# Causal attention feeding a two-layer MoE: pinned order with MoE matmuls between the attention parts, shared PSUM banks, contiguous Q/K copies

## The chip, the cores and the metric

The kernel runs on one core of one Trainium2 chip. The metric is the device time of one execution in microseconds (us), given as the median of several executions. Every experiment was timed in turns with the kernel before on the same chip. PE is TensorE (its matmuls), PEld its weight loads, DVE is VectorE, ACT ScalarE, POOL GpSimd, SP SyncE. "Clock" is the mean TensorE clock that the records say was granted, where 1.00 is full speed. A matmul is called "warm" when 512 columns take 216 ns from start to start, as they do in the tail of these traces, and "cold" when they take twice that (426 ns). PSUM is the memory that this kernel's matmuls write to; the program hands it out in banks, and has a bank written anew only when the last reader of its old content is done.

## The reference

```python
B, H, S, Nb, D = (8, 8, 576, 16, 64)
k_all = np.concatenate([beacon_k, k], axis=2)          # 16 beacon rows ahead of 576
v_all = np.concatenate([beacon_v, v], axis=2)
scores = scale * np.matmul(q, k_all.transpose(0, 1, 3, 2))
scores = np.where(causal, -1000000000.0, scores)       # beacon columns are never masked
a = np.exp(scores - scores.max(-1, keepdims=True))
a /= a.sum(-1, keepdims=True) + 1e-09
x = np.matmul(a, v_all).transpose(0, 2, 1, 3).reshape(B * S, H * D)   # 4608 x 512
h = x @ w_in                                           # 512 -> 2048
out = np.maximum(0.01 * h, h) @ w_out                  # 2048 -> 512
```

Two heads make a *pair*; there are 32 pairs. The MoE works on chunks of 512 tokens. A *step* of the steady part does one pair of attention, 16 MoE matmuls of the first layer (moe1: four groups of four) and 16 of the second (moe2: one sum of 16).

## The kernel before

Only what the change and the argument touch; "..." marks cuts.

```python
ps_sc = ... tile_pool(name="ps_sc", bufs=2, space=PSUM)    # scores, 2 banks each
ps_mb = ... tile_pool(name="ps_mb", bufs=2, space=PSUM)    # Q, K, x transposes and values
ps_acc = ... tile_pool(name="ps_acc", bufs=2, space=PSUM)  # MoE sums
...
def load_beacon_k(b):                                      # for each of 8 batches
    for e in range(2):
        nc.gpsimd.dma_start(out=bk[:, e, :], in_=beacon_k[b]...)   # casting load
    ps = ps_mb.tile(...); nc.tensor.transpose(ps[:, 0:128], ...); nc.vector.tensor_copy(out=bkT[:, b]..., in_=ps[:, 0:128])
...
def transposes(g):
    ...
    for par in range(2):
        nc.gpsimd.tensor_copy(out=kT[ps_, 0:NB], in_=bkT[ps_, b, 2 * hp + par, :])
    for src, dst in ((q_nat, qT), (k_nat, kT[:, NB : NB + S])):
        ps = ps_mb.tile([128, 1024], BF16, name="mb", tag="mb")
        for i in range(RI):                                # RI = 6 transposes of 96 rows
            nc.tensor.transpose(...)
        nc.vector.tensor_copy(
            out=dst.rearrange("c (p i) -> c i p", i=RI),   # writes hop by 6 elements
            in_=ps[:, 0:S].rearrange("c (i p) -> c i p", i=RI),
        )
...
for g in range(NG + 2):
    ...                       # loads of the next batch, two weight pieces
    transposes(g)
    if 1 <= g <= NG:
        scores(g - 1)         # 4 parts: 12 matmuls, exp on ACT
    if g >= 2:
        values(g - 2)         # 30 matmuls in two halves, x_nat, 5 transposes, copy to xT
    if g >= NPAIR + 2:
        moe_step(g - NPAIR - 2)   # 4 x moe1 (4 matmuls, Prelu on ACT), then moe2 (16 matmuls)
for m in range(NG - NPAIR, NPAIR * (NCH + 1)):
    moe_step(m)               # 12 steps of MoE alone: the tail
```

The order of the instructions on each engine is not this program order: a scheduler decides it. It puts nearly all MoE matmuls at the end of a step and leaves one or two between attention parts.

The softmax here doesn't subtract the row's maximum and nothing guards it: scores larger than these inputs give would overflow.

## Time and profile before

| | before |
|---|---|
| time, median of 4 runs beside the kernel after | 523.54 us (521.84 to 524.33) |
| span of the profiled execution | 522.0 us |
| mean granted clock | 0.928 |
| PE busy | 407.5 us, so 114.5 us idle |
| first step with moe2 begins at | 128.28 us |

To read it, cut the span in two at the begin of the first step that has both MoE layers. Up to there is the *start* (128.3 us), after it the *rest* (393.7 us): 24 steps with attention and both MoE layers, the last two short of a part, and the tail of 12 steps of MoE alone. The first is TensorE's largest waits over the whole execution (total us, times, longest us); the second the rows of the page for PE and its clock, in 40 slices of the span; the third the two copies:

```profile
PE mb L261 <- DVE qT L187: 35.3, 29, 1.5
PE mb L148 <- DMA bk<-in_beacon_k_dram: 34.0, 2, 17.5
PE mb L261 <- DVE kT L187: 21.9, 24, 1.1
PE sc L204 <- POOL kT L178: 6.7, 1, 6.7
```

```profile
PE   0103777887888888888888888888987889999996
PEclk9999999987888887998888998888799889999999
```

Of the 114.5 us that TensorE is idle, 57 are waits of the value matmuls for the bank that a Q or K copy still reads, and 41 (34.0 and 6.7) belong to the beacon at the start. The two copies themselves (busy us, mean ns):

```profile
L187 DVE COPY qT<-mb 128x576 bf16<-128x576 bf16 x32 | 66.4, 2075 | 9.6 <-PE mb L182 7.2
L187 DVE COPY kT<-mb 128x576 bf16<-128x576 bf16 x32 | 70.4, 2199 | 0.0
```

The clock row dips in most slices of the middle and stays up only in the tail.

### The profile page before, as it was taken

How to read it: one execution, taken by the hardware profiler on the slowest of the kernel's cores; microseconds unless marked ns; L12 is line 12 of the kernel's file. 1: busy time of each engine (PE TensorE's matmuls, PEld its weight loads, DVE VectorE, ACT ScalarE, POOL GpSimd, SP SyncE). 2: the span in 40 equal slices, each digit the busy share in tenths (PEclk: the TensorE clock that was granted, in tenths of full speed). 3: DMA queues.
4: the chain of work that ended last, by engine and by line, in shares of the span. 5: the costliest groups of instructions: out<-in, count | busy, mean ns of one | idle time of the engine just before them, and what ended most of it. 6: DMA issues, size and time to landing. Idle time of an engine off the chain costs nothing.

```text
span 522.0 us, 7381 instructions
## 1 busy us (share of the span) xinstructions
PE 407.5 (78%) x3048; PEld 208.6 (40%) x3048; DVE 239.3 (46%) x369; ACT 201.0 (39%) x305; POOL 115.7 (22%) x205
## 2 busy tenths in 40 slices
PE   0103777887888888888888888888987889999996
PEld 0102435443444444444444444444444445444443
DVE  1305768655455556555554556454355443100111
ACT  0001364555344443444444444534344345333310
POOL 4944344514050405031500331030000000000000
PEclk9999999987888887998888998888799889999999
DMA  9999946537070626217430700070000001011112
GB/s 217 204 266 193 175 95 43 103 88 49 1 202 21 57 35 164 60 27 65 121 102 21 67 21 21 20 68 21 0 23 35 5 21 41 21 41 40 41 40 82
DMA packets 63713, 38.10 MB, mean 73 GB/s; under 512 B 42688, under 2 KB 59072, under 8 KB 63680
## 3 DMA queue, kind: packets, MB, share of 16 engines
q0 software_dynamic: 45184, 9.31, 21.6%
q1 hardware_dynamic: 18496, 28.32, 19.2%
q8 instruction: 24, 0.39, 0.3%
q14 instruction: 9, 0.07, 0.0%
HBM read 37.49 MB, written 9.44 MB: 90 GB/s over the span
## 4 chain that ended last, share of the span: by engine, by line
PE 63%; DVE 24%; DMA 7%; issue 3%; ACT 1%; SPq 1%; POOL 0%; DVEq 0%; POOLq 0%
PE acc L293 26%; PE acc L305 24%; DVE kT L187 12%; DVE qT L187 9%; PE mb L261 7%; DMA bk<-in_beacon_k_dram 4%; PE sc L204 3%; PE mb L279 3%; DVE osb L313 2%; DMA v_aug<-in_v_dram 2%; DMA k_raw<-in_k_dram 1%; PE mb L182 1%; ACT aT L215 1%; SPq L131 1%; DVE aT L232 0%
## 5 line engine op out<-in xcount | busy, mean ns | idle before, releaser
L215 ACT ACTIVATE aT<-sc 128x928 bf16<-128x928 f32 (+2 forms) x128 | 105.3, 856 | 187.1 <-PE sc L204 186.8
L293 PE MATMUL acc<-xT,w_in_sb 128*128 128x512 bf16 x576 | 165.9, 423 | 0.0
L305 PE MATMUL acc<-w_out_sb,gT 128*128 128x512 bf16 x576 | 129.5, 379 | 0.0
L300 ACT ACTIVATE gT<-acc 128x512 bf16<-128x512 f32 x144 | 86.0, 597 | 112.5 <-PE acc L293 112.5
L313 DVE COPY osb<-acc 128x512 f32<-128x512 f32 x36 | 24.9, 692 | 188.6 <-PE acc L305 188.6
L261 PE MATMUL mb<-v_aug,aT 128*128 128x65 bf16 (+1 forms) x960 | 56.7, 217 | 64.6 <-DVE qT L187 35.3
L293 PEld LDWEIGHTS <-w_in_sb 128*128 128x128 bf16 x576 | 59.0, 108 | 63.7 <-issue 24.1
L305 PEld LDWEIGHTS <-gT 128*128 128x128 bf16 x576 | 56.4, 98 | 67.9
L261 PEld LDWEIGHTS <-aT 128*128 128x128 bf16 (+1 forms) x960 | 48.2, 112 | 82.9 <-issue 79.1
L187 DVE COPY qT<-mb 128x576 bf16<-128x576 bf16 x32 | 66.4, 2075 | 9.6 <-PE mb L182 7.2
L187 DVE COPY kT<-mb 128x576 bf16<-128x576 bf16 x32 | 70.4, 2199 | 0.0
L178 POOL COPY kT<-bkT 64x16 bf16<-64x16 bf16 x64 | 12.7, 199 | 198.1 <-PE sc L204 100.8
L204 PE MATMUL sc<-qT,kT 64*128 64x128 bf16 (+5 forms) x384 | 50.0, 335 | 8.2 <-POOL kT L178 6.7
L271 DVE TENSOR_TENSOR x_nat<-mb,rec 128x384 bf16<-128x384 f32 x64 | 31.3, 490 | 2.0
L137 POOL CAST q_nat<-q_raw 96x768 bf16<-96x768 f32 x28 | 22.7, 828 | 39.5 <-issue 38.8
L137 POOL CAST k_nat<-k_raw 96x768 bf16<-96x768 f32 x32 | 27.7, 889 | 5.9 <-DMA k_raw<-in_k_dram 5.9
L148 PE MATMUL mb<-ident,bk 128*128 128x128 bf16 x8 | 1.9, 242 | 34.0 <-DMA bk<-in_beacon_k_dram 34.0
L279 PE MATMUL mb<-ident,x_nat 128*128 128x128 bf16 (+1 forms) x160 | 24.9, 272 | 0.7 <-DVE x_nat L271 0.7
L204 PEld LDWEIGHTS <-kT 64*128 64x128 bf16 (+1 forms) x384 | 14.0, 105 | 28.3 <-issue 15.7
L279 PEld LDWEIGHTS <-x_nat 128*128 128x128 bf16 (+1 forms) x160 | 15.3, 126 | 18.9 <-DVE x_nat L271 10.5
L270 DVE RECIPROCAL rec<-mb 128x6 f32<-128x6 f32 x64 | 12.2, 190 | 23.3 <-PE mb L261 23.3
L160 POOL DMA_DIRECT2D v_aug<-in_v_dram x24 | 21.2, 893 | 4.7 <-DMA w_in_sb<-in_moe_w_in_dram 4.7
(28 smaller groups left out, 166.5 us busy)
## 6 DMA issues: line engine op xcount, KB each, us to landing
q_raw<-in_q_dram SPq DMA_DIRECT2D x32, 288.0 KB, 4.0
k_raw<-in_k_dram SPq DMA_DIRECT2D x32, 288.0 KB, 4.7
out_dram<-osb SPq DMA_DIRECT2D x36, 256.0 KB, 2.0
v_aug<-in_v_dram POOLq DMA_DIRECT2D x24, 128.0 KB, 4.9
w_in_sb<-in_moe_w_in_dram POOLq DMA_DIRECT2D x4, 512.0 KB, 19.6
w_out_sb<-in_moe_w_out_dram POOLq DMA_DIRECT2D x4, 512.0 KB, 13.8
v_aug<-in_v_dram POOLq DMA_DIRECT2D x8, 112.0 KB, 3.5
v_aug<-in_v_dram POOLq DMA_DIRECT2D x8, 80.0 KB, 4.5
```

The costliest lines, as they stand in the source:

```text
L137: eng.tensor_copy(out=dst[:, :, h0 + 2 * e : h0 + 2 * e + 2, :], in_=raw[:, 2 * e : 2 * e + 2].rearrange("p h i d -> p i h d"),)
L160: nc.gpsimd.dma_start(out=t[:, c, :, 0:D], in_=v[b, :, OFF[c] : OFF[c] + 128].rearrange("h p d -> p h d"),)
L187: nc.vector.tensor_copy(out=dst.rearrange("c (p i) -> c i p", i=RI), in_=ps[:, 0:S].rearrange("c (i p) -> c i p", i=RI),)
L204: nc.tensor.matmul(out=sc[0 : ROWS[c], par, col - c0 : col - c0 + w], lhsT=kT[ps_, c * 128 : c * 128 + ROWS[c]], rhs=qT[ps_, q0 : q0 + w], ...
L215: nc.scalar.activation(out=aT[:, :, c0 : c0 + w], in_=sc[:, :, 0:w], func=AF.Exp, scale=0.125)
L261: nc.tensor.matmul(out=avv[:, n, 0 : D + 1], lhsT=aT[0 : ROWS[c], par, a0 : a0 + 128], rhs=va[0 : ROWS[c], c, 2 * hp + par, :], start=(c = ...
L271: nc.vector.tensor_tensor(out=x_nat[:, t0:t1].rearrange("p t e d -> p (t e) d"), in0=avv[:, :, 0:D], in1=rec[:, n0:n1, None].to_broadcast( ...
L279: nc.tensor.transpose(ps[:, q0 : q0 + rows], x_nat[0:rows, t].rearrange("p e d -> p (e d)"), ident[0:rows, 0:rows],)
L293: nc.tensor.matmul(out=acc, lhsT=w_in_sb[:, j, fc * 128 : (fc + 1) * 128], rhs=xT[:, j, i * 512 : (i + 1) * 512], start=(j == 0), stop=(j ...
L300: nc.scalar.activation(out=gT[i][:, fc, :], in_=acc, func=AF.Prelu, alpha=0.01)
L305: nc.tensor.matmul(out=acc, lhsT=gT[i][:, fc, t * 128 : (t + 1) * 128], rhs=w_out_sb[:, fc, :], start=(fc == 0), stop=(fc == NF - 1),)
L313: nc.vector.tensor_copy(out=osb, in_=acc)
```

## The change

Its intent is to keep TensorE busy without gaps. It has five parts:

1. *Order.* The whole schedule is pinned to program order, and eight groups of four MoE matmuls stand between the attention parts of a pair. Q and K stay one pair ahead of the scores, as before, but the first pair is now transposed before the loop, so every pair comes one earlier against the weight loads.
2. *Banks.* The two PSUM pools of two banks become one pool of four single banks.
3. *Copies.* The Q/K copies write contiguously and take the hop on the PSUM side.
4. *Beacon K.* One plain load, one cast by POOL and eight transposes up front take the place of 16 casting loads.
5. *First loads.* Two heads first, and one load for each tensor.

```diff
-    ps_mb = ...(name="ps_mb", bufs=2, ...)
-    ps_acc = ...(name="ps_acc", bufs=2, ...)
+    ps_one = ...(name="ps_one", bufs=4, ...)
...
-    def load_beacon_k(b):
-        for e in range(2):
-            nc.gpsimd.dma_start(out=bk[:, e, :], in_=beacon_k[b].rearrange("h n d -> (h n) d"))
+    def load_beacon_k():
+        nc.scalar.dma_start(out=bk_raw, in_=beacon_k.rearrange("b h n d -> (h n) b d"))
+        nc.gpsimd.tensor_copy(out=bk, in_=bk_raw[:, :, None, :].to_broadcast([128, B, 2, D]))
...
-                out=dst.rearrange("c (p i) -> c i p", i=RI),
-                in_=ps[:, 0:S].rearrange("c (i p) -> c i p", i=RI),
+            out=dst.rearrange("c (p i) -> c p i", i=RI),
+            in_=ps[:, 0:S].rearrange("c (i p) -> c p i", i=RI),
...
+    def fill(m, n):                       # even n: one moe1 group; odd n: a quarter of moe2
+        i, part = divmod(m, NPAIR)
+        if m < 0: return
+        if n % 2 == 0:
+            if i < NCH: moe1(i, part * 4 + n // 2)
+        elif i >= 1: moe2(i - 1, part, n // 2)
...
+    order = tc.manual_schedule(engines={PE, Activation, DVE, Pool, SP})
+    with order:
...
+        for g in range(NG + 1):
+            m = g - NPAIR - 1
...
+            if has(g + 1): t_q(g + 1, 0)          # Q transposes and copy, one pair ahead
+            fill(m, 0)
+            if has(g + 1): t_q(g + 1, 1)          # K; its beacon columns copied by POOL
+            fill(m, 1)
+            if has(g): score(g, 0); score(g, 1)
+            fill(m, 2)
+            if has(g - 1): value(g - 1, 0)
+            fill(m, 3)
+            if has(g): score(g, 2); score(g, 3)
+            fill(m, 4)
+            if has(g - 1): value(g - 1, 1)
+            fill(m, 5)
+            fill(m, 6)
+            if has(g): masks(g)
+            if has(g - 1): x_transposes(g - 1)
+            fill(m, 7)
```

(Shortened: engine names stand without their prefix, and short conditions on one line.)

## The prediction

> **What bounds the kernel now.** I read the page's chain first, then the waits of TensorE in the steady part, then one table of stretches, then single instructions. The chain that ended last:
>
> ```profile
> PE 63%; DVE 24%; DMA 7%; issue 3%; ACT 1%; SPq 1%; POOL 0%; DVEq 0%; POOLq 0%
> PE acc L293 26%; PE acc L305 24%; DVE kT L187 12%; DVE qT L187 9%; PE mb L261 7%; DMA bk<-in_beacon_k_dram 4%; PE sc L204 3%; PE mb L279 3%; DVE osb L313 2%; DMA v_aug<-in_v_dram 2%; DMA k_raw<-in_k_dram 1%; PE mb L182 1%; ACT aT L215 1%; SPq L131 1%; DVE aT L232 0%
> ```
>
> The reader is to see that VectorE is busy only 46% of the span, yet two of its copies (Q and K out of PSUM, L187) are 21% of the chain. Why TensorE stands behind them is in its waits between 145 and 430 us:
>
> ```profile
> PE mb L261 <- DVE qT L187: 27.1, 21, 1.4
> PE mb L261 <- DVE kT L187: 19.0, 21, 1.0
> ```
>
> The value matmuls (L261) do not read qT or kT of that pair: they wait for the *bank*. The pool "mb" has two banks, and Q transposes, K transposes, two value halves and the x transposes take turns in it. So each step has 46.1/21 = 2.2 us of idle TensorE. Next, five consecutive steps and one stretch of the MoE tail (columns: stretch, length, busy us of PE, PEld, DVE, ACT, POOL, granted clock, DMA share, GB/s):
>
> ```profile
> 242.90:256.90 14.00, 11.75 (x91) 6.18 (x91) 7.05 (x13) 5.93 (x10) 4.30 (x7) 0.87 0.16 49
> 256.90:270.80 13.90, 11.56 (x91) 6.06 (x91) 8.30 (x13) 6.01 (x10) 3.08 (x5) 0.87 0.59 160
> 270.80:286.20 15.40, 13.67 (x96) 6.89 (x96) 7.05 (x14) 6.88 (x12) 0.78 (x4) 0.79 0.05 18
> 286.20:298.50 12.30, 9.87 (x87) 5.16 (x87) 7.14 (x13) 4.94 (x7) 4.72 (x6) 1.00 0.84 71
> 298.50:311.20 12.70, 10.32 (x91) 5.27 (x91) 7.08 (x13) 6.05 (x10) 4.30 (x7) 1.00 0.06 22
> 448.20:455.20 7.00, 7.00 (x34) 3.14 (x33) 0.69 (x1) 2.39 (x4) 0.00 (x0) 1.00 0.10 39
> ```
>
> The same step takes 12.3 to 12.7 us where the clock is 1.00 and 13.9 to 15.4 us where it falls to 0.79 to 0.87; the tail, with no waits, holds 1.00. So the waits cost twice: once as idle time, once through the clock that falls after them. Single pieces of the chain agree:
>
> ```profile
> 92.89 2.13 PE acc L293 x5
> ...
> 260.40 2.37 PE acc L293 x11
> ...
> 278.21 3.47 PE acc L305 x16
> ```
>
> 2.13/5 = 426 ns per 512-column matmul (cold, and the granted clock of that slice reads 9 all the same), 2.37/11 = 216 ns and 3.47/16 = 217 ns (warm). The start is another stage: up to 50 us TensorE is almost idle. The weight and V loads on POOL's queue set it; the last piece is
>
> ```profile
> 49.59 0.74 POOL L113 DMA_DIRECT2D w_out_sb<-in_moe_w_out_dram  x1 [1.92 <-DMA w_out_sb<-in_moe_w_out_dram]
> 50.38 0.45 POOL L178 COPY kT<-bkT 64x16 bf16<-64x16 bf16 x2
> ```
>
> The beacon columns of kT are copied by POOL behind loads that wait for older loads.
>
> **What the Trainium skill says.** "TensorE: Matmul & The Clock Gate", section "Wait — 56ns, not 53.3ns?", gives 426.7 ns cold and about 215.7 ns warm for N=512; the trace agrees (426 and 216). Its section "HAM oscillation — how this bites in real kernels" has gaps re-throttle the array; the table above shows it, though here waits of 1.0 to 1.4 us, two in a step, are enough. "VectorE: DVE Perf Modes", section "What auto-detection actually checks", wants step 1 in every tensor for two elements per cycle. The old Q/K copies step 6 elements in the output, the new ones 96 in the input, so neither should get it. "SBUF — State Buffer", section "Door 1: The DMA port swizzle" (note on cachelines), says that hops off a 16-byte line are penalised; the old copy's 2069 ns for 576 elements (3.6 ns each), against 457 ns for the contiguous xT copy, fits that. No page says what a strided PSUM read costs VectorE.
>
> **The change part by part.**
>
> 1. *Order of TensorE.* Old: all 16 + 16 MoE matmuls stand nearly in one block at the end of a step, and the attention parts follow each other with only 1 or 2 MoE matmuls between. New: eight groups of four, one between any two attention parts. TensorE's work per step, from start-to-start times in 266 to 290 us at full clock: 32 MoE matmuls x 0.216 = 6.91; Q and K transposes 0.26 + 0.35; scores 0.52 + 0.30 + 0.25; 30 values x 0.03 = 0.90; x transposes 0.28; sum 9.77 us. I add 0.1 for the switch into the 64-row score matmuls: 9.9.
>
> 2. *PSUM banks.* Old 2 + 2, new 4 shared, one of which the moe2 sum holds through most of the step. I listed from the built order whom each first user of a bank waits for, and put times on a step that starts at 0. The first moe1 group ends at 1.1, moe2 starts at 1.5, scores at 2.3 to 2.9. The second moe1 group (2.9) waits for the Q copy: the osb copy (0.69) ends at 0.9, then the Q copy, so it must take under 2 us. Third moe1 group (5.5): waits for the K copy, so the two must take under 4.6 us together. Score 3 (4.9) waits for the first exp: 2.8 + 1.02 = 3.8. Second value half (6.3) waits for the Prelu behind two exps: 2.8 + 1.02 + 0.94 + 0.60 = 5.4. x transposes (8.6) wait for a Prelu (7.9) and for x_nat (7.7). Every wait ends before TensorE arrives, the narrowest by some 0.6 us. So nearly the whole 2.2 us goes, and with it the cold clock. ACT has 3.79 + 4 x 0.60 = 6.2 us per step, VectorE 5 to 6; neither is the bound.
>
> 3. *Q/K copies.* 64 copies at 2.07 to 2.20 us. New: one element per cycle would be, as an estimate, double the element part of the xT copy: 457 + 300 = 0.76 us (300 ns for 576 elements at two per 0.96 GHz cycle, the rate from the VectorE page). That is 64 x 1.4 = 88 us less VectorE work, of which little lies on the end once the order is new: by part 2 the limits are about 2 us a copy. It shortens the pairs that run without MoE at the start.
>
> 4. *Start.* Beacon K comes by one plain load, cast by POOL, instead of 16 casting loads of 0.56 us each. That removes the first and second beacon waits (34 us of idle TensorE), but the pair after them waits for POOL behind V and weights as before: the same bytes through the same queue, about 51 us. The new order prepares kT one pair ahead, so pair 3 rather than 2 starts there. From there: two attention-only pairs at cold clock, 7 us each (65 us); first MoE step, warming up, 9 us; three moe1-only steps at 7.1 (TensorE 6.4, one wait for exp): 95 to 96 us. Before, the step with the first moe2 began at about 128 us (it reaches its moe2 at 139.2).
>
> 5. *Tail.* Twelve MoE-only steps, 448.2 to 518.1 = 69.9 us, at full clock already: unchanged. After it 3.9 us.
>
> Sum: 96 + 22 x 10.1 (9.9 and 0.2 for what I missed) + 9.4 + 8.4 (last two steps without Q/K, then without scores) + 69.9 + 3.9 = 410 us of span; the timed median is 1.6 above the span (523.6 against 522.0): **411 us**. The gain of 112 us is about 32 in the start and 80 in 24 steps of 13.1 on average.
>
> **The rivals.**
>
> *The strided PSUM read is as slow as the strided write.* For: every read hops 192 bytes. Then VectorE has 8 us per step and the second moe1 group waits 0.1 to 0.3 us; the start gets about 8 us longer: 415 to 425.
>
> *Shared banks become the new wait.* For: four banks serve ten tiles per step, and one is held by moe2; a Prelu stands behind 2 us of exp in ACT's queue. Against: part 2's margins. With 1 us of wait per step and a falling clock: 435 to 450.
>
> *POOL sets the pace in the steps that load Q/K.* kT's beacon columns now stand behind casts of a load issued in the same step: issue at 1.4, landing about 6 to 8.4 (288 KB took 4.0 to 4.7 us), casts of 1.65 and 1.78, so ready at about 10.7, needed at 12.1 in the next step. If late by 1 us in half the steps: +12 us.
>
> *The start stays DMA-bound and nothing else moves* (a gain hidden anyway): the DMA row reads 9 for the first four slices. I took this in already; worse ordering of POOL's queue could add 5 us.
>
> *TensorE cannot hold full clock at full load.* Against: 70 us of tail at 1.00.
>
> **Range and chances.** Low end 398: the start 9 us shorter and no 0.2 per step (411 - 9 - 4.4). High end 436: 1 us more in each of 24 steps. Rivals one to three move it by 5 to 40 us upward, the good surprises by 10 downward. Only a slip in the order that stalls every step by over 3.5 us would cancel the gain: faster 0.97, within 2% 0.02, slower 0.01.
>
> **What would show each step.** Part 1: steps of 9.8 to 10.3 us and a clock of 1.00 from about 80 us on. Part 2: no TensorE wait above 3 us in total per line in the steady part. Part 3: the Q/K copies at 0.7 to 1.0 us; near 2 us is rival one. Part 4: the first moe1 near 65 us and the first moe2 near 97. Part 5: the tail 69.9 us. Steps alternating between 10 and 11 us with a score wait on POOL would be rival three; a step above 11 us everywhere makes the prediction wrong.

## The result, and the profile after

The kernel after takes **400.41 us** (median of 4 runs, 399.46 to 401.34) against 523.54 us of the kernel before on the same chip. The ratio is 0.7651, with a 95% interval of 0.7621 to 0.7682. A ratio here is the mean time of one kernel's fast runs over that of the other's of the same rounds, so it is not quite the ratio of the medians quoted. The profiled run is a fast one, with a span of 397.9 us and a clock of 0.999.

The chain that ended last, by engine:

```profile
PE 79%; DMA 9%; DVE 3%; POOL 3%; issue 2%; ACT 2%; SPq 0%; POOLq 0%
```

VectorE had 24% of the chain and has 3%; TensorE has 79% of a shorter one. TensorE's four largest waits over the whole execution, and below them all those between 100 and 320 us:

```profile
PE sc L214 <- POOL kT L186: 22.4, 3, 13.2
PE tp L149 <- POOL bk L141: 6.3, 1, 6.3
PE av L279 <- DMA v_aug<-in_v_dram: 2.9, 1, 2.9
PE sc L214 <- ACT aT L225: 2.0, 6, 0.7
```

```profile
PE acc L315 <- DVE xT L306: 0.6, 1, 0.6
PE acc L331 <- DVE osb L340: 0.2, 1, 0.2
```

Every wait of size is in the start; the steady 220 us hold 0.8 us of listed waiting. Two consecutive steps and a stretch of the tail (length, busy us of PE, PEld, DVE, ACT, POOL, granted clock, DMA share, GB/s), and the rows by slice:

```profile
190.02:199.82 9.80, 9.69 (x94) 5.06 (x93) 4.78 (x11) 5.64 (x9) 0.00 (x0) 1.00 0.07 27
199.82:209.63 9.81, 9.71 (x94) 5.07 (x93) 5.09 (x11) 5.64 (x9) 2.76 (x2) 1.00 0.62 149
330.00:337.00 7.00, 6.95 (x34) 3.16 (x33) 0.69 (x1) 2.39 (x4) 0.00 (x0) 1.00 0.11 40
```

```profile
PE   2167068999999999999999999999999999999996
PEclk9999999999999999999999999999999999999999
```

A step is 9.80 us long and TensorE is busy for all but 0.1 of it, at full clock, whether Q and K are loaded in it or not. The copies, from the groups by line (busy us, mean ns):

```profile
L196 DVE COPY kT<-tp 128x576 bf16<-128x576 bf16 x32 | 24.1, 753 | 2.4 <-PE sc L214 0.5
L196 DVE COPY qT<-tp 128x576 bf16<-128x576 bf16 x32 | 23.9, 745 | 0.0
```

They took 2199 and 2075 ns before. In the account of the whole span TensorE is busy 353.9 us instead of 407.5 (the same matmuls, faster by 53.6 us) and idle 44.0 us instead of 114.5 (70.5 us less); the sum is the 124.1 us by which the span fell. So some 40% of the gain is matmuls that run at full speed, and 60% is idle time. (The trace of after lacks 51 of 3048 matmul records. Kernels with the same steps and all records, a_dvekt and a_banks22, have 359 to 361 us busy, which would make it 38 to 39% and 61 to 62%.) By stage, the start fell from 128.3 to 90.5 us (37.8) and the rest from 393.7 to 307.4 (86.3).

### The profile page after: what moved, and what is told of

It reads as the page before. It is cut to its first block, busy times and chain, and to the rows that moved or that the text cites. A ratio compares the mean times of both kernels' runs of the same rounds, so it can differ in the third digit from the quotient of the medians.

```text
span 397.9 us, 7236 instructions
## 1 busy us (share of the span) xinstructions
PE 353.9 (89%) x2997; PEld 185.0 (47%) x3048; DVE 168.7 (42%) x362; ACT 191.2 (48%) x305; POOL 103.5 (26%) x161
## 4 chain that ended last, share of the span: by engine, by line
PE 79%; DMA 9%; DVE 3%; POOL 3%; issue 2%; ACT 2%; SPq 0%; POOLq 0%
PE acc L315 31%; PE acc L331 30%; PE av L279 7%; PE sc L214 7%; DMA w_out_sb<-in_moe_w_out_dram 5%; DMA k_raw<-in_k_dram 4%; PE tp L191 3%; ACT aT L225 2%; PE tp L301 2%; DVE aT L238 1%; POOL k_nat L131 1%; POOL v_aug L165 1%; DVE x_nat L289 1%; DVE aT L251 0%; DVE xT L306 0%
## 5 line engine op out<-in xcount | busy, mean ns | idle before, releaser
L315 PE MATMUL acc<-xT,w_in_sb 128*128 128x512 bf16 x558 | 147.5, 380 | 1.9 <-DVE xT L306 0.7
L322 ACT ACTIVATE gT<-acc 128x512 bf16<-128x512 f32 x144 | 86.3, 599 | 116.0 <-PE acc L315 114.8
L214 PE MATMUL sc<-qT,kT 64*128 64x128 bf16 (+5 forms) x384 | 41.2, 312 | 24.6 <-POOL kT L186 22.4
L340 DVE COPY osb<-acc 128x512 f32<-128x512 f32 x36 | 24.8, 690 | 69.3 <-PE acc L331 66.9
L131 POOL CAST q_nat<-q_raw 96x1536 bf16<-96x1536 f32 x15 | 22.0, 1464 | 105.2 <-DMA q_raw<-in_q_dram 104.9
L279 PE MATMUL av<-v_aug,aT 128*128 128x65 bf16 (+1 forms) x960 | 43.0, 200 | 2.9 <-DMA v_aug<-in_v_dram 2.9
L289 DVE TENSOR_TENSOR x_nat<-av,rec 128x384 bf16<-128x384 f32 x64 | 31.4, 491 | 2.2
L131 POOL CAST k_nat<-k_raw 96x1536 bf16<-96x1536 f32 (+1 forms) x16 | 23.9, 1491 | 8.2 <-DMA k_raw<-in_k_dram 7.2
L196 DVE COPY kT<-tp 128x576 bf16<-128x576 bf16 x32 | 24.1, 753 | 2.4 <-PE sc L214 0.5
L196 DVE COPY qT<-tp 128x576 bf16<-128x576 bf16 x32 | 23.9, 745 | 0.0
L238 DVE TENSOR_TENSOR aT<-aT,mask 128x224 bf16<-128x224 bf16 x32 | 16.1, 502 | 9.6 <-ACT aT L225 9.6
L245 DVE TENSOR_TENSOR aT<-aT,mask 128x768 bf16<-128x768 bf16 x32 | 18.9, 590 | 0.8 <-ACT aT L225 0.8
L306 DVE COPY xT<-tp 128x576 bf16<-128x576 bf16 x32 | 14.5, 453 | 9.9 <-PE tp L301 9.8
## 6 DMA issues: line engine op xcount, KB each, us to landing
w_out_sb<-in_moe_w_out_dram POOLq DMA_DIRECT2D x4, 512.0 KB, 15.6
```

Source lines behind the costliest of these rows:

```text
L131: eng.tensor_copy(out=dst[:, :, hs, :], in_=raw[:, 0:nh].rearrange("p h i d -> p i h d"),)
L196: nc.vector.tensor_copy(out=dst.rearrange("c (p i) -> c p i", i=RI), in_=ps[:, 0:S].rearrange("c (i p) -> c p i", i=RI),)
L214: nc.tensor.matmul(out=sc[0 : ROWS[c], par, col - c0 : col - c0 + w], lhsT=kT[ps_, c * 128 : c * 128 + ROWS[c]], rhs=qT[ps_, q0 : q0 + w], ...
L238: nc.vector.tensor_tensor(out=aT[:, :, 0:112], in0=aT[:, :, 0:112], in1=tri[:, None, 16:128].to_broadcast([128, 2, 112]), op=ALU.mult,)
L279: nc.tensor.matmul(out=avv[:, n, 0 : D + 1], lhsT=aT[0 : ROWS[c], par, a0 : a0 + 128], rhs=va[0 : ROWS[c], c, 2 * hp + par, :], start=(c = ...
L289: nc.vector.tensor_tensor(out=x_nat[:, t0:t1].rearrange("p t e d -> p (t e) d"), in0=avv[:, :, 0:D], in1=rec[:, n0:n1, None].to_broadcast( ...
```

## The experiments

All outputs are right. The time is the median of all four runs, the ratio is from the fast ones; the spans and the cut into start and rest are from the profiled runs:

| kernel | what it is | time, us | ratio to before | span | start | rest |
|---|---|---|---|---|---|---|
| before | | 523.54 | 1 | 522.0 | 128.3 | 393.7 |
| after | | 400.41 | 0.7651 | 397.9 | 90.5 | 307.4 |
| b_copy | before + new copies | 426.86 | 0.8135 | 425.3 | 102.6 | 322.7 |
| a_oldcopy | after with old copies | 407.08 | 0.7764 | 405.5 | 95.0 | 310.5 |
| a_block | after, MoE in one block | 461.22 | 0.8768 | 461.5 | 100.6 | 360.9 |
| a_block_oldcopy | the same, old copies | 536.01 | 1.0227 | 534.4 | 110.7 | 423.7 |
| a_three | a_block, 3 groups of 8 moved | 402.98 | 0.7685 | 401.4 | 92.9 | 308.5 |
| a_banks22 | after, banks parted 2 + 2 | 405.10 | 0.7729 | 402.5 | 95.1 | 307.4 |
| a_sched | after, order not pinned | 399.18 | 0.7621 | 395.8 | 89.8 | 306.0 |
| b_beacon | before + plain beacon load | 510.94 | 0.9734 | 509.4 | 114.0 | 395.4 |
| b_two | b_copy + b_beacon | 419.08 | 0.7992 | 415.1 | 92.4 | 322.7 |
| b_three | b_two + kT beacon by VectorE | 411.94 | 0.7866 | 410.0 | 84.0 | 326.0 |
| a_dvekt | after + kT beacon by VectorE | 387.92 | 0.7391 | 385.6 | 78.6 | 307.0 |
| a_sched_dvekt | a_sched + the same | 393.93 | 0.7497 | 398.4 | 92.3 | 306.1 |

The profiled runs of a_block and a_sched_dvekt were each over 1.5% above the fastest of their kernel and so count as slow; no argument below rests on a difference of that size (7.4 and 9.9 us above the fastest) in them alone. The four runs of a_block lie between 455.75 and 463.19.

The prediction credited the order and the shared banks with the end of the bank wait, and gave the copies little. What the total cannot tell is which of these parts does it, whether one would do alone, and what still holds the start. (Part 5, the first loads, was not run by itself.) The texts name a theory and its rivals by letters and say for each run what they expect of it. Several runs change one thing each, so that the parts can be set against each other both in the old kernel and in the new.

### Which part removes the waits: copies or order

**b_copy**: the kernel before with only the copies' access patterns swapped. The order on TensorE stays the same, instruction for instruction: the two traces have the same 3048 matmuls in the same order.

```diff
-                out=dst.rearrange("c (p i) -> c i p", i=RI),
-                in_=ps[:, 0:S].rearrange("c (i p) -> c i p", i=RI),
+                out=dst.rearrange("c (p i) -> c p i", i=RI),
+                in_=ps[:, 0:S].rearrange("c (i p) -> c p i", i=RI),
```

> The kernel before with only the Q/K copies changed (contiguous output, strided PSUM read); TensorE's order is the same instruction for instruction. Theory A (in the old order the value matmuls stand behind these copies for a bank, so their length is on the path there): the copies take 0.75 us, the 2.2 us of bank waits per step fall under 0.5, the clock of the steps goes to 0.95 or more, steps of about 10.7 us, time 440 to 465. Rival B (only the order counts, the next wait, score on exp, takes the place of the copies): 495 to 515.

Measured: 426.86 us, ratio 0.8135 (0.8101 to 0.8169), below both ranges, so the copies alone do more than either theory gave them. TensorE's longest waits of the whole execution are now

```profile
PE mb L148 <- DMA bk<-in_beacon_k_dram: 34.1, 2, 17.7
PE sc L204 <- POOL kT L178: 7.4, 1, 7.4
PE sc L204 <- ACT aT L215: 1.5, 4, 0.7
```

and the two lines of 57 us are gone. A step is

```profile
228.49:238.96 10.47, 10.35 (x93) 5.27 (x92) 4.50 (x11) 5.74 (x9) 0.38 (x2) 1.00 0.19 34
```

at full clock. So two short strings of the diff, in the old order and the old banks, bring 97 of the 123 us. The waits and the cold clock went together, with nothing else changed. With the old copies the bank came back 1.0 to 1.4 us too late; the new copies are 1.3 to 1.4 us shorter each.

**a_oldcopy**: the opposite, the kernel after with the old patterns.

```diff
-            out=dst.rearrange("c (p i) -> c p i", i=RI),
-            in_=ps[:, 0:S].rearrange("c (i p) -> c p i", i=RI),
+            out=dst.rearrange("c (p i) -> c i p", i=RI),
+            in_=ps[:, 0:S].rearrange("c (i p) -> c i p", i=RI),
```

> The changed kernel with the old Q/K copies (strided SBUF write, 2.07 to 2.20 us). Theory A (in the new order TensorE meets the banks late enough, limits about 2 us for one and 4.6 us for both copies): steps of 9.8 to 10.2 us, the start 3 to 8 us longer, time 403 to 418. Rival C (the shorter copies carry the gain in either order): over 440.

Measured: 407.08 us, ratio 0.7764 (0.7738 to 0.779), in the range of theory A. 4.4 of the 7.6 us of span lie in the start, the other 3.1 in the rest, where steps are 9.87 us and the Q copy is waited for 6 times, 1.7 us in all. So the new order does hide copies of 2.1 us, nearly whole: the two parts stand in for each other. Either takes the steady waits away without the other, and their gains must not be added: in the rest of the span b_copy gains 71.0 us, a_oldcopy 83.2 and both together 86.3. (Over the whole run a_oldcopy gains 116 us, but that includes what the other parts of the change do for the start.)

**a_block**: the kernel after, pinned, banks and copies new, but all 32 MoE matmuls of a step in one block at its end.

```diff
-            fill(m, 0)          # and the seven others between the parts
...
             if has(g - 1): x_transposes(g - 1)
-            fill(m, 7)
+            for n in (0, 2, 4, 6, 1, 3, 5, 7):
+                fill(m, n)
```

> The changed kernel, order still pinned, but each step's 32 MoE matmuls in one block after the attention parts. Theory A (the groups between the parts hide the latencies of exp, masks and x_nat): an attention part of 5.2 us with about 2.3 us of waits, then 6.9 us of MoE, 12.1 us if the clock holds and up to 13.5 if it falls: 455 to 490. Rival E (a pinned order with one pair of lead and short copies is enough): 400 to 420.

Measured: 461.22 us, ratio 0.8768 (0.8705 to 0.8831). The pinned order without the spreading is worse than the scheduler's order of b_copy, which keeps one or two MoE matmuls between the parts. The waits between 150 and 320 us are

```profile
PE sc L214 <- ACT aT L225: 12.2, 27, 0.5
PE tp L301 <- DVE x_nat L289: 8.0, 14, 0.6
```

that is two waits for an exp and one for x_nat in each step, 0.45 + 0.46 + 0.58 = 1.5 us. Two steps of this kernel:

```profile
185.90:197.60 11.70, 10.21 (x92) 5.47 (x91) 4.51 (x11) 5.74 (x9) 3.25 (x4) 1.00 0.48 125
232.70:246.10 13.40, 11.91 (x93) 5.90 (x92) 4.50 (x11) 5.74 (x9) 3.26 (x4) 0.87 0.45 109
```

The waits are the same in both steps to 0.01 us; in the second, the 16 moe1 matmuls after them took 5.30 us instead of 3.62. So 1.5 us of waits in three pieces is at the border here: after some of them part of the matmuls run cold, after others none.

**a_block_oldcopy**: the same with the old copies, the fourth corner (the edits of a_block and of a_oldcopy together).

> a_block (pinned order, all 32 MoE matmuls in one block at the end of a step) with the old Q/K copies. Theory S (short copies and spread MoE matmuls stand in for each other: with neither, VectorE's 4.1 us of copies come ahead of the x_nat and transposes that TensorE waits for between the attention parts): 475 to 515 us, steps of 12.5 to 14 us against 11.7 in a_block, TensorE waits that name the Q/K copies or a longer wait for x_nat. Rival (in the blocked order the waits are for exp and x_nat alone, so the copies are hidden): 456 to 468.

Measured: 536.01 us, ratio 1.0227 (1.0147 to 1.0307), slower than either theory had it, and no faster than the kernel before (1.5 to 3.1% slower; against a limit of 2% that counts as unclear), although it has the new banks, the new beacon load and the pin. In the timeline of TensorE (start us, duration us, what, idle before):

```profile
247.96 0.73 PE L279 MATMUL av<-v_aug,aT 128*128 128x65 bf16 x18
250.24 0.94 PE L301 MATMUL tp<-ident,x_nat 112*128 112x112 bf16 x5 [1.55 <-DVE x_nat L289]
250.97 6.12 PE L315 MATMUL acc<-xT,w_in_sb 128*128 128x512 bf16 x16
256.93 3.62 PE L331 MATMUL acc<-w_out_sb,gT 128*128 128x512 bf16 x16
```

VectorE does the two copies (2.08 and 2.21 us) ahead of x_nat, so the wait for x_nat grows from 0.58 to 1.55 us, and the moe1 matmuls after it take 4.72 us in one step and 6.12 in the next. The step is 14.2 and 15.6 us long. Its waits are 1.0 us longer than a_block's, but the step is 2.5 to 3.9 us longer than a_block's undisturbed one: the rest is cold matmuls. My expectation had counted the wait and too little of this multiplier.

The four corners of the rest of the span, then, are: spread and new copies 307, spread and old 310, block and new 361, block and old 424 us. The copies are worth 3 us in one order and 63 in the other.

**a_three**: was it the block as such, or only the three places where it leaves TensorE waiting? Three groups go back, two ahead of the score part that waits for an exp, one ahead of the x transposes; 20 matmuls stay in one block.

```diff
             if has(g - 1): value(g - 1, 0)
+            fill(m, 0)
+            fill(m, 2)
             if has(g): score(g, 2); score(g, 3)
             if has(g - 1): value(g - 1, 1)
+            fill(m, 4)
...
-            for n in (0, 2, 4, 6, 1, 3, 5, 7):
+            for n in (6, 1, 3, 5, 7):
```

> a_block with three of its eight groups of four MoE matmuls moved out of the block, to the two places where a_block's TensorE waits 0.45 + 0.46 us for an exp (two groups, 1.7 us) and 0.57 us for x_nat (one group, 0.86 us); five groups, 20 matmuls, stay in one block. Theory (the block costs what TensorE waits at these places and the cold matmuls that follow, not the block as such): steps of 9.8 to 10.2 us at a granted clock of 1.00 against 11.7 and 13.4 in a_block, 402 to 416 us. Rival (all groups have to be spread, because a long block leaves ACT's Prelu calls or the PSUM banks behind and moves the waits elsewhere): steps of 10.8 us or more, 430 to 461 us.

Measured: 402.98 us, ratio 0.7685 (0.7657 to 0.7714). The step:

```profile
102.71:112.51 9.80, 9.80 (x92) 5.20 (x91) 4.53 (x11) 5.53 (x9) 0.38 (x2) 1.00 0.08 28
```

This is the theory's number. The block does no harm (the time is within 1% of after's). What has to be filled are the places where TensorE would wait, 1.5 us in a step of 9.8.

**a_sched**: the kernel after without the pin, so that the scheduler may reorder.

```diff
-    with order:
+    if True:
```

> The changed kernel without the pinning: the scheduler may reorder. In the built program TensorE's order differs only in the first pairs; POOL's loads and VectorE's copies move more. Theory A (it is the order as written that counts, not the pin): 393 to 410. Rival F (the pin itself is needed): over 425.

Measured: 399.18 us, ratio 0.7621 (0.7585 to 0.7657): the same as after. The order on TensorE differs only in the first pairs (among the first 300 of 3048 matmuls). It is the place of the groups in the program that counts; for the change as it stands the pin is not needed. The starts are alike (89.8 and 90.5 us) by coincidence, though, for TensorE waits there for other things: without the pin the 22.4 us of waiting for POOL's kT copies become 1.1, and those for V grow from 2.9 to 10.1.

```profile
PE av L279 <- DMA v_aug<-in_v_dram: 10.1, 3, 5.8
PE sc L214 <- POOL kT L186: 1.1, 2, 0.8
```

### Shared banks

**a_banks22**: the kernel after with the banks parted again, two for the MoE sums and two for the others.

```diff
-    ps_one = ...(name="ps_one", bufs=4, ...)
+    ps_one = ...(name="ps_one", bufs=2, ...)
+    ps_acc = ...(name="ps_acc", bufs=2, ...)
```

> The changed kernel with the four PSUM banks parted again, two for the attention tiles and two for the MoE sums. Theory A (each wait ends before TensorE arrives, with the order of the groups alone): 400 to 406, steps of 9.8 to 10.0. Rival D (the shared pool is what removes the bank waits): steps of 11 us or more, over 425.

Measured: 405.10 us, ratio 0.7729 (0.7705 to 0.7753). The rest of the span is 307.4 us, equal to after's, and no wait is listed in it. The 4.6 us are all in the start: there the Q and K transposes wait 4.6 us, in five waits, for the bank that an xT copy still reads. So the shared banks help where no MoE uses the other two, and do nothing in the steady part.

### The start

**b_beacon**: the kernel before with one plain beacon load and one cast by POOL.

```diff
-        for e in range(2):
-            nc.gpsimd.dma_start(out=bk[:, e, :], in_=beacon_k[b]...)
+        if b == 0:
+            nc.scalar.dma_start(out=bk_raw, in_=beacon_k.rearrange("b h n d -> (h n) b d"))
+            nc.gpsimd.tensor_copy(out=bk_all, in_=bk_raw[:, :, None, :].to_broadcast(...))
+        bk = bk_all[:, b]
```

> The kernel before with only the beacon loads changed: one plain load and one POOL cast for all batches in place of 16 casting loads. Theory (it removes the 34 us in which TensorE waits for beacon K, but the pairs after it stand behind the V and weight loads on POOL's queue as before): 510 to 522. Rival (the waits for beacon K are the start's bound): 490 to 505.

Measured: 510.94 us, ratio 0.9734 (0.9702 to 0.9767). That is in the theory's range. The start falls by 14.3 us, mostly because the 34.0 us of beacon waits give way to 12.4 us for POOL's cast and 11.5 instead of 6.7 us for the kT copies; the rest does not gain (395.4 against 393.7 us).

**b_two**: the edits of b_copy and b_beacon together.

> Kernel before with two small edits together: contiguous Q/K copies and the plain beacon load with one POOL cast; the old order stays to the scheduler. Theory S (the order itself is worth the step length only: 10.47 us a step in b_copy against 9.81 us after, about 24 steps = 16 us, and the beacon edit is worth the 13 us it was worth alone): 408 to 420 us, first moe2 at 96 to 101 us against 109.6 in b_copy, steps still 10.4 to 10.5 us. Rival 1 (pinned order worth nothing once both edits are in): 396 to 404. Rival 2 (the beacon gain is lost because POOL's queue of V and weights sets the start anyway): 422 to 430.

Measured: 419.08 us, ratio 0.7992 (0.794 to 0.8044), in the upper part of the theory's range. Its start is 92.4 us, 1.9 more than after's, and its steps are 10.47 us. So what the rest of the change (order, banks, first loads) still adds to two small edits is 19 us, of which 15 are 0.67 us a step. Those 0.67 us are not listed as waits: in b_copy's step TensorE counts as busy for 10.35 us. In its timeline the short groups between the parts take 0.1 to 0.3 us more from start to start than their matmuls need, at four places (a single MoE matmul 0.49 and 0.32 us instead of 0.22). I take these for waits too short to be listed, but no run shows it.

**a_dvekt**: the longest wait in the start of after is one of 13.2 us for POOL's copy of kT's beacon columns, which stands in POOL's queue behind weight loads:

```profile
51.60 0.74 POOL L111 DMA_DIRECT2D w_out_sb<-in_moe_w_out_dram  x1 [2.03 <-DMA w_out_sb<-in_moe_w_out_dram]
52.38 0.94 POOL L186 COPY kT<-bkT 64x16 bf16<-64x16 bf16 x4
52.63 1.25 PE L214 MATMUL sc<-qT,kT 64*128 64x512 bf16 x4 [13.16 <-POOL kT L186]
```

The experiment gives that copy to VectorE.

```diff
-                nc.gpsimd.tensor_copy(out=kT[ps_, 0:NB], in_=bkT[ps_, b, 2 * hp + par, :])
+                nc.vector.tensor_copy(out=kT[ps_, 0:NB], in_=bkT[ps_, b, 2 * hp + par, :])
```

> The changed kernel with the beacon columns of kT copied by VectorE rather than POOL. Theory G (the pair that starts at 52.6 us waits for nothing but POOL's queue, which stands behind the V and weight loads): it starts near 40 us, the first moe1 near 52 rather than 64, the steps stay at 9.8, time 386 to 392. Rival H (the start is bound by the loads themselves, so the wait moves to V or to the weights): 396 to 402.

Measured: **387.92 us** (386.83 to 388.43), ratio 0.7391 (0.7364 to 0.7418), as theory G had it, 11.3 us below a_sched and the fastest of all. The start falls from 90.5 to 78.6 us and the first moe1 from 64.0 to 46.85 us. What TensorE waits for now is V and the first casts:

```profile
PE av L279 <- DMA v_aug<-in_v_dram: 7.8, 7, 3.7
PE tp L149 <- POOL bk L141: 6.2, 1, 6.2
PE tp L191 <- POOL q_nat L131: 2.3, 1, 2.3
```

**b_three**: b_two with the same edit.

```diff
-            nc.gpsimd.tensor_copy(out=kT[ps_, 0:NB], in_=bkT[ps_, b, 2 * hp + par, :])
+            nc.vector.tensor_copy(out=kT[ps_, 0:NB], in_=bkT[ps_, b, 2 * hp + par, :])
```

> b_two and also the beacon columns of kT copied by VectorE instead of POOL. Theory G (POOL's queue holds that copy back in the start, as in a_dvekt, where it was worth 12.5 us): 396 to 410 and 7 us or more below b_two. Rival (in the old order the scheduler places VectorE's small copies in front of work that TensorE waits for, or the wait for V takes the place of the wait for POOL): within 4 us of b_two, 408 to 420.

Measured: 411.94 us, ratio 0.7866 (0.7813 to 0.792). It is 7.1 us below b_two, as the theory asked, but misses its 396 to 410. The start falls by 8.4 us, while the rest grows by 3.3: some steps are 11.2 us long instead of 10.5. In the steps at 94.5 and 137.3 us VectorE's two kT copies (0.87 us together) stand between the two halves of x_nat, and the transposes of the second half wait 0.47 us for it. So the rival was right about the steps, and the theory about the start. That the wait is the whole 0.7 us of such a step is not shown. With the same three small edits the old order (with the old banks and first loads) stays 24 us behind a_dvekt.

**a_sched_dvekt**: a_dvekt without the pin (the edits of a_sched and a_dvekt together).

> After without the pinned order and with the beacon columns of kT copied by VectorE. The two gains touch the same wait at the start (no pin: 1.2 us, VectorE copy: 12.5 us). Theory: 384 to 389 us, same as a_dvekt within 1%. Rival (the scheduler orders the first pairs differently and moves the V wait): 390 to 400.

Measured: 393.93 us (390.32 to 400.21), ratio 0.7497 (0.7431 to 0.7564): the rival's range. The fast runs lie between 390.32 and 394.68 us, and the intervals of this ratio and of a_dvekt's (0.7364 to 0.7418) do not overlap, so here the pin is worth some 6 us. The profiled run counts as slow, so the cause stays open. What its trace shows is a rest as short as a_dvekt's (306.1 and 307.0 us) and 19.2 us of waits for V in the start against 7.8; that would be the rival's V wait, but no fast run has a trace to confirm it. The theory, that the two edits touch the same wait and the pin is idle, fails for this pair: a_sched had already lost that wait.

## Why the prediction was right, point by point

*The total* was 411 us against a measured 400.4; the range held it. The mechanism in the steady part was right as far as it went (the waits go and the clock comes back), its credit to the parts was not, and two terms of the sum were too large.

*Order and banks (parts 1 and 2).* The sum gave 9.77 us, and with its two additions 10.1. Measured: 9.80 us. That the bare sum comes so close is in part luck. The switch into the scores is real: four MoE matmuls ahead of a score group take 0.96 us to the next start instead of 0.86, twice in a step. But the K transposes (0.26 us, not 0.35) and the last two score parts (0.45, not 0.55) had been read in the old order, where K stands right ahead of the scores and the two parts stand apart, so a part of the switch was in them already. From 90.5 us to the last attention step's end at 324.9 us are 234.4 us, where the sum had 22 x 10.1 + 9.4 + 8.4 = 240: 5.6 us of the error. The margins, the narrowest 0.6 us, held but for two waits, 0.8 us in 220 us, and the clock was 1.00 as the step predicted.

What this step did not see is how many ways lead there. It put the end of the bank wait down to the order and the banks and gave the copies "little". a_oldcopy confirms that for the new order, but b_copy shows that the copies alone would have ended it in the old one, and a_banks22 that the shared banks have no part in it in the steady steps.

*Copies (part 3).* The estimate of 0.76 us met 745 and 753 ns: the strided PSUM read fits the one element per cycle of that estimate, so the first rival fell. The cited section of "VectorE: DVE Perf Modes" has a second way to two elements per cycle, with source and destination both in SBUF; these copies read PSUM, so the conclusion stands.

*Start (part 4).* The wait for POOL behind V and weights was right, as was its place: 52.6 us against 51. The first moe1 came at 64.0 against 65, by luck: the wait ended 1.6 us later than predicted, and the two attention-only pairs after it took 11.2 us together (52.6 to 63.8), not 14. The other mis-sized term is what follows: "first MoE step, warming up, 9 us; three moe1-only steps at 7.1". The four took 26.7 us, 6.6 to 6.8 each, not 30.3. The array was warm already: in the attention-only pairs a Q transpose group takes 0.69 us at 57.9 us and 0.42 us at 63.8 us. So the first full step began at 90.5 and not at 96: the other 5.5 us, 3.6 of them from these four steps. Together, 411 - 5.6 - 5.5 = 400.

*Tail (part 5).* 69.3 us from 324.9 to 394.2, predicted 69.9.

*The split of the gain*, about 32 in the start and 80 in the steps, came out as 37.8 and 86.3. (The 24 old steps averaged 13.3 us, 319.9 us in all, not the 13.1 that the prediction has; its 80 fits the 13.3.)

*The rivals.* Slow strided reads: refuted (753 ns). Shared banks as a new wait: refuted. POOL as the pace of the loading steps: not seen in after, whose loading steps are as long as the others; in a_three it appears as 1.3 us in all. TensorE not holding full clock: refuted, 1.00 for 300 us. The start bound by transfers: half right. What held it was not the transfers' rate but one small copy behind them in POOL's queue, as a_dvekt shows with 12 us; I had named that queue as the cause and left it in the sum as fixed.

## What to carry to other kernels

Two remedies for one wait do not add: test each alone before crediting either, because here two access patterns brought 97 of the 123 us, and all the other parts without them 116. An idle microsecond of TensorE can cost more than itself when the matmuls after it run cold (1.0 us more of waiting made a step 2.5 to 3.9 us longer in a_block_oldcopy), so find the few places where it would wait and put just enough independent matmuls there; three groups of four did within 1% what eight did. And keep a tiny copy that TensorE needs off a queue that holds large loads.

## What the Trainium skill lacked or had wrong

- "TensorE: Matmul & The Clock Gate", section "HAM oscillation — how this bites in real kernels", ties the fall of the clock to idle gaps above about 3.4 us. The section after it, "A second HAM failure mode: psum-queue depth-cycling", has frequent micro-idles between groups of matmuls do it too, but gives no lengths. Here gaps much shorter than 3.4 us do it when several come close together: with 0.45 + 0.46 + 0.58 us in some 5 us the next 16 matmuls took 3.62 us in one step and 5.30 us in another, and with 0.45 + 0.46 + 1.55 us they took 4.72 and 6.12 us.
- The granted clock of the records is no proof of warm matmuls. In the kernel before it reads 1.00 from 92.8 to 95.1 us, where five matmuls of 512 columns took 2.13 us, 426 ns each and twice the warm time. "TensorE: Matmul & The Clock Gate", section "Seeing it yourself", warns that the throttle events of a trace can be unreliable; it gives no case of a full reading over cold matmuls.
- No page gives the cost of a strided PSUM read by VectorE; it would belong to "PSUM — Partial Sum Buffer". A copy of 128 x 576 bf16 that hops 192 bytes in PSUM and writes contiguously took 745 to 753 ns, against 453 ns for the fully contiguous one of the same size.
- "SBUF — State Buffer", section "Specifications (TRN2)", says that each hop to a new 16-byte line pays a penalty, without a size for compute engines. A bf16 write by VectorE at a step of 12 bytes took 2075 to 2199 ns for 576 elements, 2.8 to 2.9 times the new copy, which writes contiguously and hops in its PSUM read instead.
